# The last chunk's output blocks share PSUM banks, a bias moves to VectorE, and the softmax sums become halving additions

## The chip, the cores and the metric

The kernel runs on one core of a Trainium2 chip. The metric is the device time of one execution in microseconds. A difference of about 0.2%, some 0.4 us, is what a measurement of this kernel can tell from no change.

## The reference

```python
S, D, F, H = 2048, 640, 1536, 32          # Dh = 20; window W = 8, dilation 2
xn  = layernorm(x)                        # A_x; no scale, no shift
q, k, v = split(xn @ wqkv)                # 32 heads of 20
# position s attends to s, s-2, ..., s-14; those before 0 are masked
attn = softmax(einsum("bhsd,bhswd->bhsw", q, kg) * Dh**-0.5)
A    = einsum("bhsw,bhswd->bhsd", attn, vg).reshape(B, S, D) @ wo
B    = gelu(xn @ w1 + b1) @ w2 + b2       # tanh form
out  = x + A + B                          # bf16 in and out
```

## The kernel before

The 2048 rows are cut into four chunks of 512 (`NCH`, `CH`), each of four blocks of 128 rows (`BPC`). For each chunk the kernel normalizes the rows, turns them (a transposing DMA from SP for chunks 1 to 3, the `td` pieces named `tc`), and makes q, k and v by matmuls (`pj`, and `hj` in chunk 0) which ScalarE copies out of PSUM (`pc`, `hc`). The columns of a q, k or v tile are reordered so that a head has four rows in each of five tiles of 128.

Attention of a window of eight is done elementwise on VectorE. `qk` multiplies q by shifted k into two buffers, `half[0]` and `half[1]`, four window positions each. Some of the five tiles are then added up on VectorE, `pa` (two tiles onto two others) and `pb` (another tile onto the first), and `lg` sums over the rest with matmuls against `head_of`, 32 output rows each, into the PSUM tile `L`. How many tiles VectorE adds is `LEVEL[n]`: at level 0, 1, 2 and 3, `lg` has 40, 24, 16 and 8 matmuls. Then the softmax: `m` (maximum), `mx` (subtract), `ex` (exp on ScalarE), `ss` (sum over the eight positions), `ri` (reciprocal as Exp(-Ln) on ScalarE), `at` (multiply). `xd` and `xs` spread the result over the rows of a head by DMAs from SP, for blocks 0, 1 and 2, 3. `av` multiplies by v, `ad` and `ot` add up into `oT`. Chunk 0's softmax goes in two halves of 64 columns (`PARTS`).

The MLP's first product is `f1`, its GELU on ScalarE `ge`. ScalarE changes its table between GELU and the exp/ln functions.

For chunks 0 to 2 the output is made turned: `t{n}{s}{pc}` accumulates 128 output columns `s` over the 12 tiles of the MLP (pc 0 to 3) and the five of `oT` (pc 4), `u` adds the bias on ScalarE, `ut` turns it by a DMA from SP, `ud` adds it into the output by an accumulating DMA from POOL. x was stored there before (`xp`). For chunk 3 the output is made straight, by blocks of 128 rows: `o3{bl}{pc}` accumulates 512 low columns (`lo`) and 128 high ones (`hi`) in two PSUM tiles, ScalarE copies both (`oc`), and POOL adds them into the output (`od`), where `xp3` had stored x and `xb3` had added the bias b2. The last block, `LASTB`, is not stored first: `xl` adds b2 to its x in SBUF, `o33` makes its low columns, `oclo` adds x to them on VectorE and stores them from SP, `ohi` makes the high columns, 17 matmuls, `ochi` adds x and `ochd` stores them from ScalarE's queue.

PSUM has three pools: `psA`, four buffers (tag `acc`, for the projections and `f1`), `psO`, two (tag `o`, for the output), and `psL`, one of two banks (tag `L`, for the logits).

The order of all this on TensorE, VectorE, ScalarE and SP is written out by hand: `ORDER` is a list of 609 pieces, and each engine's queue gets its instructions in that order and runs them in that order. POOL's queue is left to the framework. Waits between engines are put in by the framework, tile by tile.

The end of the list before:

```python
... t244 u24 o312 ut23 o313 ud22 ud23 ot3 o320 o321
o322 o323 o324 oc32 od32 ut24 o314 oc31 od31 o300 o301 o302 o303 o304 o332 o333 o334 ud14 ohi ud24 oc30 od30 oclo ochi
ochd
```

Of the kernel before, what the change touches and what calls it, by code (L numbers as in the profile page):

```python
# [42 lines left out]
tp01a gb3 tp01b tc01a tc01b gb4 gd gc0 ge tb b1 hj102 gc1 ho st02a st02 st03a hc102 gc4 st03 hj101 rs02 xn02 rs03 xn03  # L43
st10a st12a st13a st11a hc101 st12 hj100 hc100 hj200 tp02 tc02 tp03 tc03 pk st13 hj201 hc200 st11 st10 hj202 hc202
hj012 hc012 hc201 rs1 rc1 hj112 hc112 xn12 tc12 xn10 hj210 qk000 hj011 hc011 tc10 hj110 hc110 qk001 hj010 hc010 hc210
hj111 hc111 qk011 qk010 pa011 pa001 xn11 tc11 xn13 hj211 hc211 f10_5 tc13 f10_4 ge0_4 ge0_5 f10_0 ge0_0 f10_7 f10_10
pj113 pc113 pj103 pj111 ge0_10 pj101 pc111 pj114 ldx ge0_7 pa000 pc101 pa010 lg0 mask m0a ld2 pc103 pj102 pc114 pad11
su21 mx0a ex0a pj112 pc112 m0b mx0b ss0a pc102 ex0b ri0a ss0b pj100 pc100 at0a ri0b at0b pj110 pj104 pc104 pc110 xd0
qk111 f10_2 ge0_2 su22 qk100 hj212 hc212 f10_6 ge0_6 pj121 su20 f10_1 pc121 su23 ldo f11_10 ge1_10 ng2 ge0_1 sq20
f11_5 f10_11 pj122 pc122 f10_3 qk110 sq22 t040 qk101 f11_0 t000 lg1 xp0 av010 ge0_3 sq21 xs0 ge1_0 sq23 rs2 f10_8  # L50
ge0_8 t001 m1 f11_3 rc2 xn23 tc23 ge0_11 av031 t041 mx1 av021 xn20 tc20 f11_7 av011 ge1_5 ge1_7 av001 ge1_3 xp1 f10_9
t042 t002 xn21 ge0_9 tc21 pj120 xn22 tc22 av030 av000 f11_9 ge1_9 pj124 ex1 av020 ss1 pc120 pc124 pj123 pc123 ad00 ri1
t043 f11_2 t003 pj204 at1 pc204 xd1 su31 ad01 pad12 ad02 ot0 pj200 pc200 pj201 pc201 av101 xp2 pj212 su30 pc212 pj220
pj213 pc220 pc213 pj223 pc223 pj211 su33 pc211 pj203 su32 ng3 sq33 pad21 av100 sq31 pj202 f11_6 t004 u00 av110 xs1
av130 t044 av120 av131 av121 t010 av111 t011 t012 t013 u04 t020 t014 sq32 pc203 pc202 pj221 sq30 rs3 rc3 ad11 u01 ut00
ad10 ad12 t030 pj210 pc221 t031 t021 t022 ut01 ge1_2 pj214 xn33 tc33 t032 t033 t034 xn31 tc31 ge1_6 pj224 t023 t024
f11_8 ot1 pc214 pad22 pc210 qk201 qk211 qk210 xn30 tc30 f12_9 qk200 f11_1 pa210 pa201 xn32 ge1_8 u02 pa211 pa200 f11_4
ge1_1 t100 ge1_4 tc32 pj311 pc311 pb212 ud00 ud01 ge2_9 pj310 pc310 pad31 pj304 pc304 pj314 pc314 t101 pj300 pj324
pc324 ut02 pj303 f12_10 pb202 pc224 u03 pc303 xp3 pj301 pc301 xl ge2_10 pc300 f13_9 pj313 pc313 pj312 ud02 ut03 ud03
pj302 pc302 f13_6 ge3_6 pj323 lg2 pc312 qk300 m2 pc323 f11_11 ge1_11 f13_0 ge3_0 mx2 ut04 f13_11 ge3_9 ex2 pa300 ss2  # L60
qk310 ri2 at2 xs2 qk301 t130 t131 f12_1 ge2_1 ge3_11 t132 f13_10 qk311 t102 t103 f13_2 pa310 xd2 t104 pj320 pc320
f13_1 ge3_1 u10 ut10 ud10 f12_8 pa311 pa301 pb312 ge2_8 f13_8 ge3_8 t110 t133 t111 t112 t113 t114 u11 ge3_10 f12_5
pj222 pc222 pj321 pc321 pb302 lg3 av200 t134 u13 m3 av221 ge2_5 xb3 f12_11 t140 t141 t120 ut11 mx3 f12_2 ge3_2 av211
ex3 ss3 ri3 av220 ge2_2 f13_5 ge2_11 t142 t143 t121 t122 t123 f12_6 ge2_6 at3 xs3 f12_3 ge2_3 t124 u12 f12_7 pj322
ud04 av210 av201 av231 f12_0 t144 ge2_7 ge2_0 t200 av230 pc322 u14 ut12 ud11 f12_4 ge2_4 ge3_5 f13_4 ge3_4 o310 f13_7
ge3_7 t210 ad20 ad21 ad22 ot2 f13_3 t201 t202 pad32 av321 t203 ge3_3 o311 av331 ut13 av320 xd3 t204 u20 av300 ut14
ut20 ud12 ud13 t211 t212 t240 t213 t214 av311 u21 ud20 t241 t242 av310 av330 t220 t221 t222 t223 t224 u22 ut21 t243
av301 ad30 ad31 o330 o331 t230 ad32 t231 t232 t233 t234 u23 ut22 ud21 t244 u24 o312 ut23 o313 ud22 ud23 ot3 o320 o321
o322 o323 o324 oc32 od32 ut24 o314 oc31 od31 o300 o301 o302 o303 o304 o332 o333 o334 ud14 ohi ud24 oc30 od30 oclo ochi
ochd  # L70
# [4 lines left out]
def kernel(  # L75
# [544 lines left out]
    def do_o(n, bl, pc, parts):  # L620
        cs = slice(bl * P, (bl + 1) * P)
        if pc == 0 and "lo" in parts:
            for part in ("lo", "hi"):
                pool, tag = (psA, "acc") if bl % 2 else (psO, "o")
                tiles[part, n, bl] = pool.tile([P, CH], F32, tag=tag, name=part)
        lo, hi = tiles["lo", n, bl], tiles["hi", n, bl]
# [4 lines left out]
        for k, (lhs, rhs) in enumerate(srcs):
            first, last = pc == 0 and k == 0, pc == 4 and k == len(srcs) - 1
            if "lo" in parts:
                nc.tensor.matmul(lo[:], lhsT=lhs, rhs=rhs[:, 0:CH], start=first, stop=last)  # L634
            if "hi" in parts:
                nc.tensor.matmul(hi[:, 0 : D - CH], lhsT=lhs, rhs=rhs[:, CH:D], start=first, stop=last)  # L636

    def do_oc(n, bl):
        osb = outp.tile([P, D], BF16, tag="osb", name="osb")
        tiles["osb", n, bl] = osb  # L640
        nc.scalar.copy(osb[:, 0:CH], tiles["lo", n, bl][:])
        nc.scalar.copy(osb[:, CH:D], tiles["hi", n, bl][:, 0 : D - CH])

    def do_od(n, bl):
        b = n * BPC + bl
        nc.gpsimd.dma_start(out_sd[b * P : (b + 1) * P, :], tiles["osb", n, bl][:], accum_op=ALU.add)
# [41 lines left out]
    last = (NCH - 1, BPC - 1)  # L688

    def do_oclo():  # L690
        osb = outp.tile([P, D], BF16, tag="osb", name="osb")
        tiles["osb", last] = osb
        nc.vector.tensor_tensor(out=osb[:, 0:CH], in0=tiles["lo", *last][:], in1=x_sb[:, LASTB, 0:CH], op=ALU.add)
        nc.sync.dma_start(out_sd[LASTB * P :, 0:CH], osb[:, 0:CH])
# [4 lines left out]

    def do_ochi():  # L700
        osb = tiles["osb", last]
        nc.vector.tensor_tensor(
            out=osb[:, CH:D], in0=tiles["hi", *last][:, 0 : D - CH], in1=x_sb[:, LASTB, CH:D], op=ALU.add
        )

    def do_ochd():
        nc.scalar.dma_start(out_sd[LASTB * P :, CH:D], tiles["osb", last][:, CH:D])
# [41 lines left out]
    for n in range(NCH):  # L749
# [52 lines left out]
        for bl in range(BPC):  # L802
            final = n * BPC + bl == LASTB
            for pc in range(5):
                piece(f"o{n}{bl}{pc}", do_o, n, bl, pc, ("lo",) if final else ("lo", "hi"))
            if not final:
                piece(f"oc{n}{bl}", do_oc, n, bl)
                piece(f"od{n}{bl}", do_od, n, bl)
# [39 lines left out]
```

## Time and profile before

| | |
|---|---|
| median of 3 runs | 210.01 us (209.93 to 210.13) |
| the profiled execution | 210.03 us, span 208.0 us |
| TensorE busy | 203.5 us, 1164 matmuls |
| VectorE busy | 180.9 us, 141 instructions |
| ScalarE busy | 127.5 us, 234 instructions |
| POOL busy | 24.9 us, 37 instructions |
| first transpose to end of the last matmul | 5.46 to 204.82 us |

The span runs from the first instruction of the program to the end of its last; some 2 us of the execution lie outside it. In a group of instructions ("L433 DVE TENSOR_TENSOR half<-qT,kT ... x16 | 44.3, 2820 | 1.0") the line is that of the kernel's source, then come the engine, what it writes and reads, how often, the microseconds of all, the nanoseconds of one, and the engine's idle time before them with what ended it. Matmuls are pipelined: the next starts before the row of the last one ends, so the price of one is the distance between starts. PE is TensorE, PEld its weight loads, DVE VectorE, ACT ScalarE, SP the SyncE queue; a small q behind an engine is its sequencer, which issues DMAs.

### The profile page before, as it was taken

Reading aid. Unit: us, or ns where it says so; the run is one execution under the profiler, and the core shown is the slowest. Engines: PE = TensorE matmul, PEld = TensorE weight load, DVE = VectorE, ACT = ScalarE, POOL = GpSimd, SP = SyncE. Lnnn points to the kernel's source line nnn. Section 1 sums busy time; section 2 is a strip of 40 time slices with the busy share of each in tenths; the row PEclk is TensorE's granted clock in tenths of the full one; section 3 lists DMA queues with packets and bytes.
Section 4 is the critical chain, followed back from the end, with each engine's and each line's share of the span. In section 5 each row is a group of like instructions: output and inputs, shape, how many; then the busy total and the mean of one; then the engine's idle time right before and its main releaser. Section 6 shows DMA issues by size and latency. Waiting matters only on the chain.

```text
span 208.0 us, 2951 instructions
## 1 busy us (share of the span) xinstructions
PE 203.5 (98%) x1164; PEld 107.0 (51%) x1164; DVE 180.9 (87%) x141; ACT 127.5 (61%) x234; POOL 24.9 (12%) x37
## 2 busy tenths in 40 slices
PE   8999999999999999999999999999999999999993
PEld 3999754554445554444455544444444444445552
DVE  2598995999699999999999989999999999999201
...
GB/s 217 388 395 137 68 207 395 60 122 238 162 82 162 11 189 138 25 50 91 90 25 56 114 123 0 0 188 81 37 0 100 121 108 54 50 50 76 49 68 63
DMA packets 36863, 23.88 MB, mean 115 GB/s; under 512 B 24946, under 2 KB 34674, under 8 KB 36850
## 3 DMA queue, kind: packets, MB, share of 16 engines
...
q8 instruction: 9, 0.15, 0.3%
q14 instruction: 4, 0.03, 0.0%
...
## 4 chain that ended last, share of the span: by engine, by line
PE 66%; DVE 21%; ACT 9%; DMA 2%; issue 1%; DVEq 0%; ACTq 0%
PE T L673 17%; PE pps L336 15%; PE hps L599 13%; PE lo L634 7%; PE gps L380 7%; DVE half L433 5%; DVE half L587 4%; DVE sums L530 3%; PE idle L446 2%; ACT L173 2%; DVE half L465 2%; DMA xnT<-xn 2%; DVE half L578 2%; ACT hT L615 2%; PE hi L636 2%; PE gps L349 1%
## 5 line engine op out<-in xcount | busy, mean ns | idle before, releaser
L599 PE MATMUL hps<-xnT,w_sb 128*128 128x512 bf16 x240 | 56.9, 379 | 0.1
L433 DVE TENSOR_TENSOR half<-qT,kT 128x5120 bf16<-128x5120 bf16 x16 | 44.3, 2820 | 1.0 <-ACT vT L400 0.7
L673 PE MATMUL T<-hT,w_sb 128*128 128x512 bf16 x180 | 43.3, 379 | 0.0
L685 POOL DMA_DIRECT2D out_dram<-x_sb x15 | 19.5, 1357 | 172.8 <-DMA x_sb<-x_sb 168.7
L599 PEld LDWEIGHTS <-w_sb 128*128 128x128 bf16 x240 | 23.3, 98 | 28.2 <-issue 1.2
L615 ACT ACTIVATE hT<-hps,bT 128x512 bf16<-128x512 f32 x36 | 24.1, 687 | 7.3 <-PE hps L599 7.2
L673 PEld LDWEIGHTS <-w_sb 128*128 128x128 bf16 x180 | 17.6, 98 | 21.1
L578 DVE TENSOR_TENSOR half<-vT,ax 128x2560 bf16<-128x2560 bf16 x16 | 23.1, 1484 | 2.4 <-PE L L479 2.4
L676 ACT ACTIVATE x_sb<-T,bT 128x512 bf16<-128x512 f32 x15 | 10.3, 687 | 23.6 <-PE T L673 23.6
L578 DVE TENSOR_TENSOR half<-vT,x_sb 128x2560 bf16<-128x2560 bf16 x16 | 22.6, 1485 | 0.0
L587 DVE TENSOR_TENSOR half<-half,half 128x5120 bf16<-128x5120 bf16 x8 | 22.3, 2820 | 0.1
L673 PE MATMUL T<-oT,wo 128*128 128x512 bf16 x75 | 18.3, 379 | 0.3 <-DVE oT L592 0.3
L336 PE MATMUL pps<-xnT,wk_sb 128*128 128x512 bf16 x75 | 18.3, 379 | 0.0
L336 PE MATMUL pps<-xnT,wv_sb 128*128 128x512 bf16 x75 | 18.3, 379 | 0.0
L336 PE MATMUL pps<-xnT,wq_sb 128*128 128x512 bf16 x75 | 18.2, 379 | 0.0
L173 ACT ACT_TABLE_LOAD x12 | 15.4, 1283 | 0.9 <-PEq L832 0.7
L465 DVE TENSOR_TENSOR half<-half 128x2048 bf16<-128x2048 bf16 x12 | 13.9, 1217 | 0.0
L336 PEld LDWEIGHTS <-wv_sb 128*128 128x128 bf16 x75 | 8.8, 117 | 7.6
L336 PEld LDWEIGHTS <-wq_sb 128*128 128x128 bf16 x75 | 8.7, 118 | 7.7 <-issue 0.4
L336 PEld LDWEIGHTS <-wk_sb 128*128 128x128 bf16 x75 | 8.8, 117 | 7.5
L263 ACT ACTIVATE xn<-x_sb,nmr,rstd 128x640 bf16<-128x640 bf16 x12 | 10.6, 916 | 3.2 <-DMA xnT<-xn 2.3
L400 ACT CAST vT<-pps 128x512 bf16<-128x512 f32 x15 | 8.5, 589 | 6.1 <-PE pps L336 6.1
...
## 6 DMA issues: line engine op xcount, KB each, us to landing
w_sb<-in_B_w_dram SPq DMA_DIRECT2D x4, 960.0 KB, 10.3
...
```

Source lines behind the costliest of these rows:

```text
L173: nc.scalar.preload_act_table_set(name)
L336: nc.tensor.matmul(ps[:], lhsT=wqkv_p[which][:, ti, to, :], rhs=xnT[:, ti, :], start=(ti == 0), stop=(ti == KT - 1),)
L380: nc.tensor.matmul(ps[:, to - a, :], lhsT=wqkv_p[which][:, ti, to, :], rhs=tiles["xnT", 0][:, ti, pair * 2 * P : (pair + 1) * 2 * P], star ...
L433: nc.vector.tensor_tensor(out=half[h][:, :, :, cs], in0=q[:, :, at].unsqueeze(1).to_broadcast([P, W // 2, KT, 2 * P]), in1=window(k, h, at ...
L465: nc.vector.tensor_tensor(out=even, in0=even, in1=odd, op=ALU.add)
L578: nc.vector.tensor_tensor(out=half[h][:, :, :, cs], in0=window(qkv_tile(n, 2), h, cs), in1=ax_view(n)[:, j, ws, :].unsqueeze(2).to_broadca ...
L587: nc.vector.tensor_tensor(out=a, in0=a, in1=b, op=ALU.add)
L599: nc.tensor.matmul(ps[:], lhsT=w1_sb[:, ti, ft * P : (ft + 1) * P], rhs=tiles["xnT", n][:, ti, :], start=(ti == 0), stop=(ti == KT - 1),)
L615: nc.scalar.activation(hT, tiles["hps", n, ft][:], ACT.Gelu_apprx_tanh, bias=bT[:, ft : ft + 1], scale=1.0)
L634: nc.tensor.matmul(lo[:], lhsT=lhs, rhs=rhs[:, 0:CH], start=first, stop=last)
L673: nc.tensor.matmul(ps[:], lhsT=lhs, rhs=rhs, start=pc == 0 and k == 0, stop=pc == 4 and k == len(srcs) - 1)
L685: nc.gpsimd.dma_start(dst, src, accum_op=ALU.add)
```

## The change

The last two blocks of chunk 3 (`DIRECT = 2`) are both finished on VectorE and stored directly: x plus bias is added as PSUM is emptied (`direct`). `dc` does this for block 2 and `dd` stores it from SP. `xl` adds the bias for two blocks, `xp3` and `xb3` cover two, and `oc32` and `od32` are gone.

The high columns of two blocks share a bank. Those of blocks 0 and 1 lie in one `psA` tile. Block 3's low columns and the high columns of blocks 2 and 3 lie in one tile `tail` of the `psL` pool: the first bank holds the low columns, the second the two high parts. Only the first matmul in a bank has the start flag.

The softmax sums (`ss`) are three additions of halves in float32 in place of one reduction: four positions onto four, two onto two, one onto one. They are kept in the `attn` tile before `at` overwrites it, or, for chunk 0, in a part of `half[0]`.

`LEVEL[3]` is 3: VectorE adds one tile more in each half (`pb304`, `pb314`), and `lg3` has 8 matmuls.

`ORDER` is written anew throughout; the counts of the other pieces stay.

```diff
+DIRECT = 2
-LEVEL = (1, 0, 2, 2)
+LEVEL = (1, 0, 2, 3)
...
     def rows(n):
-        cs = slice(n * BPC, min((n + 1) * BPC, LASTB))
+        cs = slice(n * BPC, min((n + 1) * BPC, LASTB + 1 - DIRECT))
...
     def do_xl():
-        nc.vector.tensor_tensor(out=x_sb[:, LASTB, :], in0=x_sb[:, LASTB, :], in1=b2bc[:], op=ALU.add)
+        rows_ = x_sb[:, LASTB + 1 - DIRECT :, :]
+        nc.vector.tensor_tensor(
+            out=rows_, in0=rows_, in1=b2bc[:].unsqueeze(1).to_broadcast([P, DIRECT, D]), op=ALU.add
+        )
...
     def do_sum(n, i):
-        total = softmax_tile("sums", n, [P], F32)
-        nc.vector.tensor_reduce(
-            out=total[:, i, :], in_=tiles["e", n][:, i, :, :].rearrange("p w c -> p c w"), axis=AX.X, op=ALU.add
-        )
+        a, e = sums(n, i), tiles["e", n][:, i, :, :]
+        nc.vector.tensor_tensor(out=a, in0=e[:, 0 : W // 2, :], in1=e[:, W // 2 :, :], op=ALU.add)
+        for k in (2, 1):
+            nc.vector.tensor_tensor(out=a[:, 0:k, :], in0=a[:, 0:k, :], in1=a[:, k : 2 * k, :], op=ALU.add)
...
+    def out_ps(bl, hi):
+        if bl >= BPC - DIRECT and (hi or bl == BPC - 1):
+            whole = get("tail", lambda: psL.tile([P, W, P], F32, tag="L", name="tail"))[:].rearrange("p w c -> p (w c)")
+            return whole[:, CH + (bl % 2) * P : CH + (bl % 2 + 1) * P] if hi else whole[:, 0:CH]
+        pool, tag = (psA, "acc") if hi or bl == 1 else (psO, "o")
+        key = ("hi", bl // 2) if hi else ("lo", bl)
+        ps = get(key, lambda: pool.tile([P, CH], F32, tag=tag, name=key[0]))
+        return ps[:, (bl % 2) * P : (bl % 2 + 1) * P] if hi else ps[:]
...
             if "hi" in parts:
-                nc.tensor.matmul(hi[:, 0 : D - CH], lhsT=lhs, rhs=rhs[:, CH:D], start=first, stop=last)
+                bank = bl // 2
+                first = bank not in opened
+                opened.add(bank)
+                nc.tensor.matmul(
+                    out_ps(bl, True), lhsT=lhs, rhs=rhs[:, CH:D], start=first, stop=final, skip_group_check=True
+                )
...
+    def direct(bl, hi):
+        b = (NCH - 1) * BPC + bl
+        room = half[1][:].rearrange("p w t c -> p (w t c)")[:, (bl % 2) * D : (bl % 2 + 1) * D]
+        cs = slice(CH, D) if hi else slice(0, CH)
+        nc.vector.tensor_tensor(out=room[:, cs], in0=out_ps(bl, hi), in1=x_sb[:, b, cs], op=ALU.add)
+        return room, out_sd[b * P : (b + 1) * P, :]
...
+    def do_dc():
+        direct(BPC - 2, False)
+        tiles["dc"] = direct(BPC - 2, True)
+    def do_dd():
+        room, dst = tiles["dc"]
+        nc.sync.dma_start(dst, room)
```

The parts of the new order that matter here:

```python
... at0b ri0a at0a pc110 pj100 pc100 xd0 qk101
qk110 hj212 f10_1 ge0_1 f11_0 ge1_0 su21 xs0 ... lg1 ld2 ge0_3 f11_10 sq20 rs2 ldo xp0
... pb302 pb312 pb304 ... pb314 f13_8 ge3_8 lg3 ut04 xs2 av220 m3 mx3 ex3
... t244 u24 ot3 o332 o300 o301
o302 o303 o320 o321 o322 o304 ud14 ud22 o314 o323 ut23 ut24 ud23 o324 dc o333 o334 oclo ohi oc30 od30 oc31 od31 ochi
dd ud24 ochd
```

In the list of the changed program's instructions with their waits, the first matmul of `o333` and the first of `ohi` wait for VectorE; the list of before has no such wait at either place.

More of the change, by code (lines that the diff above doesn't have):

```diff
@@ L42 @@
 pad01 pad02 st00a st00 sum1 rs00 mean1 neg1 sq1 xn00a xn00b tp00a wa tp00b wb tc00a tc00b rs01 ga xn01a xn01b gb2
[L43 to L70, printed above, removed]
+tp01a gb3 tp01b tc01a tc01b gb4 gd gc0 ge tb b1 gc1 gc4 hj101 st03a st03 rs03 st02a st02 hj102 hc102 ho hj100 xn03
+rs02 xn02 st13a st11a st13 hj201 hc101 st12a st10a hc100 tp03 tc03 tp02 tc02 hj200 hj202 hc200 hc202 hc201 hj111 hc111
@@ new lines @@
+st12 st10 st11 rs1 rc1 hj112 hc112 xn12 tc12 hj210 xn10 tc10 hj110 hc110 hj211 hc211 pk qk000 hc210 qk001 pa000 pa010
+hj011 hj012 hc012 hc011 xn11 tc11 xn13 tc13 hj010 hc010 qk010 f10_7 qk011 ge0_7 f10_5 pad11 ge0_5 f10_10 ge0_10 pa001
+f10_4 f10_0 ge0_0 pj104 pj103 pa011 ge0_4 pj111 pc111 pj114 pj101 pc103 lg0 mask pc104 m0b pc114 pc101 ldx su22 mx0b
+ex0b pj112 pc112 m0a pj102 pc102 mx0a ex0a ss0b ri0b pj113 pc113 ss0a pj110 at0b ri0a at0a pc110 pj100 pc100 xd0 qk101
+qk110 hj212 f10_1 ge0_1 f11_0 ge1_0 su21 xs0 f11_3 ge1_3 su23 qk100 f10_2 hc212 ge0_2 su20 f10_9 f11_7 ge1_7 f10_11
@@ new lines @@
+ge0_11 ng2 f10_6 ge0_6 f10_8 sq21 ge0_8 f10_3 sq23 ge0_9 sq22 qk111 pj124 lg1 ld2 ge0_3 f11_10 sq20 rs2 ldo xp0 f11_9
+av010 m1 pc124 av031 rc2 xn23 xn20 pj121 t000 tc23 pc121 f11_5 ge1_10 tc20 av030 ge1_9 t040 t041 av011 t042 av021 mx1
+av000 xn22 tc22 ge1_5 av001 av020 xn21 tc21 ex1 ss1 ad00 xp1 pj122 pj120 pc122 t001 t002 pc120 f11_11 t043 ri1 at1
+ad01 ad02 xd1 t003 ot0 pj123 pc123 pad12 xp3 pad21 av111 pj202 pj221 pc221 pc202 pj200 xp2 pj212 pc212 av101 pj203
+pc203 pj210 pc200 su31 pc210 pj220 pj224 pc224 pc220 su33 xs1 pj222 su32 pj213 pj201 pc222 pc201 su30 ng3 av110 av100
@@ new lines @@
+av130 t044 u04 pj204 pc204 pc213 av121 sq33 pj211 sq30 av131 t010 av120 t011 t012 pj223 pc223 f11_8 t013 sq32 sq31 rs3
+rc3 t004 u00 xn33 tc33 t014 u01 pj214 pad22 t020 t021 t022 t023 t030 t031 t032 pc211 t033 xn32 tc32 t024 t034 ut00
+pc214 xn31 tc31 ge1_11 f11_6 ad10 ad11 ad12 ot1 xn30 qk201 qk211 pa210 f11_1 ge1_6 ge1_1 qk210 ge1_8 f11_4 f11_2 ge1_2
+qk200 pa211 pa200 pa201 f12_3 ge2_3 tc30 pj302 pc302 pj320 pj314 pc314 ge1_4 u03 pj303 pc303 pj301 pb212 pj312 pc312
+ud00 pb202 pc301 pj313 pc313 pc320 pj310 pj300 pc300 f13_5 pj304 ge3_5 pc310 pad31 pj311 f12_9 pc311 pc304 xl f13_9
@@ new lines @@
+ge3_9 ut01 ge2_9 u02 lg2 f13_4 f12_4 qk310 m2 f13_3 ge3_3 pa301 ut02 ut03 mx2 ex2 ud01 qk300 ss2 ri2 t100 t110 pj321
+t101 t102 pa300 at2 qk311 qk301 pa311 pa310 f13_2 pb302 pb312 pb304 pc321 t111 t112 t103 t104 pad32 ud02 t113 t114
+ge3_2 f13_6 xd2 ge3_4 pj324 f12_8 u11 pc324 ge2_8 ge3_6 f13_1 ge3_1 t120 f12_11 ge2_11 u10 t121 t122 f12_10 t123
+ge2_10 f12_7 ge2_7 f13_10 pb314 f13_8 ge3_8 lg3 ut04 xs2 av220 m3 mx3 ex3 av201 ut10 t130 t131 t132 ss3 av230 ud10
+t124 u12 ut11 f12_0 ud11 t133 t134 u13 ut12 ri3 ut13 xb3 t140 ud12 t141 t142 f12_5 t143 ge3_10 at3 xd3 pj323 pc323
@@ new lines @@
+av211 ge2_0 t144 ge2_4 u14 ut14 pj322 pc322 xs3 av221 av231 av200 av210 ad20 ad21 ad22 f13_0 ud13 ud03 f12_2 ge3_0
+o330 o310 ge2_2 ge2_5 f12_1 ge2_1 ot2 f12_6 ge2_6 av331 av321 av311 f13_11 t210 o311 f13_7 t211 t212 t213 t200 t201
+t202 t203 t204 u20 o331 ut20 t214 u21 ut21 ud20 ud21 t220 t221 t222 t223 av310 ge3_7 t224 u22 ut22 t230 t231 t232 t240
+t233 t234 u23 av330 t241 t242 t243 o312 ge3_11 o313 av301 av300 ud04 av320 ad31 ad30 ad32 t244 u24 ot3 o332 o300 o301
+o302 o303 o320 o321 o322 o304 ud14 ud22 o314 o323 ut23 ut24 ud23 o324 dc o333 o334 oclo ohi oc30 od30 oc31 od31 ochi
@@ L498, in softmax_tile, with attn_tile, sums @@
         return get((key, n), lambda: smp.tile([P, PARTS[n]] + [s // PARTS[n] if s == P else s for s in shape], dtype, tag=key, name=key))
+    scratch = half[0][:].rearrange("p w t c -> p (w t c)").bitcast(F32)
     def shifted(n, i):
-        cs, width = part(n, i)
         if PARTS[n] == 1:
             return tiles["L", n][:]
-        low = half[0][:].rearrange("p w t c -> p (w t c)").bitcast(F32)[:, 0 : W * P]
-        return low.rearrange("p (i w c) -> p i w c", i=PARTS[n], w=W)[:, i, :, :]
+        return scratch[:, 0 : W * P].rearrange("p (i w c) -> p i w c", i=PARTS[n], w=W)[:, i, :, :]
+    def attn_tile(n):
+        return get(("attn", n), lambda: smp.tile([P, W, P], BF16, tag="attn", name="attn"))
+    def sums(n, i):
+        if PARTS[n] == 1:
+            return attn_tile(n)[:].rearrange("p w c -> p (w c)").bitcast(F32).rearrange("p (w c) -> p w c", w=W // 2)
+        room = scratch[:, W * P : W * P + W * P // 2]
+        return room.rearrange("p (i w c) -> p i w c", i=PARTS[n], w=W // 2)[:, i, :, :]
     def do_max(n, i):
@@ L528, in do_sum @@
     def do_sum(n, i):
-        total = softmax_tile("sums", n, [P], F32)
-        nc.vector.tensor_reduce(
-            out=total[:, i, :], in_=tiles["e", n][:, i, :, :].rearrange("p w c -> p c w"), axis=AX.X, op=ALU.add
-        )
+        a, e = sums(n, i), tiles["e", n][:, i, :, :]
+        nc.vector.tensor_tensor(out=a, in0=e[:, 0 : W // 2, :], in1=e[:, W // 2 :, :], op=ALU.add)
+        for k in (2, 1):
+            nc.vector.tensor_tensor(out=a[:, 0:k, :], in0=a[:, 0:k, :], in1=a[:, k : 2 * k, :], op=ALU.add)
     def do_recip(n, i):
         rs = get(("rs", n), lambda: smp.tile([P, PARTS[n], P // PARTS[n]], F32, tag="m", name="rs"))
-        total = tiles["sums", n][:, i, :]
+        total = sums(n, i)[:, 0, :]
         table(LOG_SET)
@@ L542, in do_attn @@
         cs, width = part(n, i)
-        attn = get(("attn", n), lambda: smp.tile([P, W, P], BF16, tag="attn", name="attn"))
+        attn = attn_tile(n)
         nc.vector.tensor_tensor(
@@ L617, in do_ge, with do_o @@
         )
[L620 to L626, printed above, removed]
+    def out_ps(bl, hi):
[6 more added lines that the diff above has]
+        return ps[:, (bl % 2) * P : (bl % 2 + 1) * P] if hi else ps[:]
+    opened = set()
+    def do_o(bl, pc, parts):
+        n, cs = NCH - 1, slice(bl * P, (bl + 1) * P)
         if pc < 4:
@@ L631, in do_o, with do_oc, do_od @@
         for k, (lhs, rhs) in enumerate(srcs):
-            first, last = pc == 0 and k == 0, pc == 4 and k == len(srcs) - 1
+            final = pc == 4 and k == len(srcs) - 1
             if "lo" in parts:
-                nc.tensor.matmul(lo[:], lhsT=lhs, rhs=rhs[:, 0:CH], start=first, stop=last)
+                nc.tensor.matmul(out_ps(bl, False), lhsT=lhs, rhs=rhs[:, 0:CH], start=pc == 0 and k == 0, stop=final)
             if "hi" in parts:
-                nc.tensor.matmul(hi[:, 0 : D - CH], lhsT=lhs, rhs=rhs[:, CH:D], start=first, stop=last)
-    def do_oc(n, bl):
-        osb = outp.tile([P, D], BF16, tag="osb", name="osb")
[L640 to L646, printed above, removed]
+                bank = bl // 2
[4 more added lines that the diff above has]
+                )
+    def do_oc(bl):
+        osb = outp.tile([P, D], BF16, tag="osb", name="osb")
+        tiles["osb", bl] = osb
+        nc.scalar.copy(osb[:, 0:CH], out_ps(bl, False))
+        nc.scalar.copy(osb[:, CH:D], out_ps(bl, True))
+    def do_od(bl):
+        b = (NCH - 1) * BPC + bl
+        nc.gpsimd.dma_start(out_sd[b * P : (b + 1) * P, :], tiles["osb", bl][:], accum_op=ALU.add)
+    def direct(bl, hi):
+        b = (NCH - 1) * BPC + bl
+        room = half[1][:].rearrange("p w t c -> p (w t c)")[:, (bl % 2) * D : (bl % 2 + 1) * D]
+        cs = slice(CH, D) if hi else slice(0, CH)
+        nc.vector.tensor_tensor(out=room[:, cs], in0=out_ps(bl, hi), in1=x_sb[:, b, cs], op=ALU.add)
+        return room, out_sd[b * P : (b + 1) * P, :]
     def spent_x(i):
@@ L685, in do_ud @@
         nc.gpsimd.dma_start(dst, src, accum_op=ALU.add)
-    last = (NCH - 1, BPC - 1)
+    def do_dc():
[4 more added lines that the diff above has]
+        nc.sync.dma_start(dst, room)
     def do_oclo():
[L691 to L694, printed above, removed]
+        room, dst = direct(BPC - 1, False)
+        nc.sync.dma_start(dst[:, 0:CH], room[:, 0:CH])
     def do_ohi():
         for pc in range(5):
-            do_o(*last, pc, ("hi",))
+            do_o(BPC - 1, pc, ("hi",))
     def do_ochi():
[L701 to L704, printed above, removed]
+        tiles["hi"] = direct(BPC - 1, True)
     def do_ochd():
-        nc.scalar.dma_start(out_sd[LASTB * P :, CH:D], tiles["osb", last][:, CH:D])
+        room, dst = tiles["hi"]
+        nc.scalar.dma_start(dst[:, CH:D], room[:, CH:D])
     pieces = {}
@@ L713, in piece @@
         pieces[name] = lambda: fn(*args)
-    for name in "tb b1 mean1 ho ldx ld2 ldo xl oclo ohi ochi ochd mask pk".split():
+    for name in "tb b1 mean1 ho ldx ld2 ldo xl dc dd oclo ohi ochi ochd mask pk".split():
         piece(name, locals()[f"do_{name}"])
@@ L802 @@
         for bl in range(BPC):
-            final = n * BPC + bl == LASTB
             for pc in range(5):
[L805 to L808, printed above, removed]
+                piece(f"o{n}{bl}{pc}", do_o, bl, pc, ("lo",) if bl == BPC - 1 else ("lo", "hi"))
+            if bl < BPC - DIRECT:
+                piece(f"oc{n}{bl}", do_oc, bl)
+                piece(f"od{n}{bl}", do_od, bl)
     engines = {getattr(mybir.EngineType, e) for e in ("PE", "DVE", "Activation", "SP")}
```

## The prediction

> **What bounds the kernel now.** I read the page first, then the waits, the chain and the timeline of the last microseconds.
>
> ```profile
> PE 203.5 (98%) x1164; PEld 107.0 (51%) x1164; DVE 180.9 (87%) x141; ACT 127.5 (61%) x234; POOL 24.9 (12%) x37
> ...
> PE   8999999999999999999999999999999999999993
> PEld 3999754554445554444455544444444444445552
> DVE  2598995999699999999999989999999999999201
> ```
>
> TensorE is busy in every slice, so what counts is its queue: the work in it and the holes in it. VectorE is nearly as full until about 193 us and can open holes. The waits say how little it does:
>
> ```profile
> DVE osb L693 <- PE lo L634: 10.2, 1, 10.2
> ACT hT L615 <- PE hps L599: 7.2, 8, 1.6
> ...
> PE T L673 <- DVE oT L592: 0.3, 1, 0.3
> ...
> PE L L479 <- DVE half L470: 0.2, 1, 0.2
> ```
>
> ScalarE and VectorE wait for TensorE for many microseconds, TensorE for VectorE for tenths. The chain prices the matmuls:
>
> ```profile
> 34.17 1.41 PE L L479 x24
> ...
> 49.20 1.09 PE pps L336 x5
> ...
> 203.86 0.96 PE hi L636 x17
> ```
>
> A 512-wide matmul takes 0.216 us (1.09/5), a logits matmul 0.059 (1.41/24), a 128-wide one 0.056 (0.96/17), and a lo/hi pair 0.272. I multiplied these by the matmuls of each piece and compared the sums with the starts in the trace: from the first transpose at 5.46 to 204.82 TensorE loses about 2.0 us. The visible holes are about 0.3 at the start, 0.44 ahead of `t004` (the output product waiting for `ot0`; the 0.3 of the waits, since a matmul's row outlasts its turn), 0.34 ahead of `lg3` (waiting for `pb302`), 0.25 ahead of `f12_3` (GELU late behind the softmax logarithm and a table load) and some of 0.1. The end:
>
> ```profile
> 203.70 0.50 PE L636 MATMUL hi<-w_sb,wq_sb 128*128 128x128 bf16 x6
> 203.95 0.69 DVE L693 TENSOR_TENSOR osb<-lo,x_sb 128x512 bf16<-128x512 f32 x1 [10.19 <-PE lo L634]
> ...
> 204.84 0.29 DVE L702 TENSOR_TENSOR osb<-hi,x_sb 128x128 bf16<-128x128 f32 x1 [0.20 <-PE hi L636]
> 205.17 0.36 ACTq L707 DMA_DIRECT2D out_dram<-osb  x1
> ```
>
> The last block's high columns (L636) start at 203.70 while VectorE empties its low columns (L693): they overlap, because `lo` and `hi` are two tiles. After the last matmul come 0.2 us, one VectorE addition, a store, and the end of the span at 208.0.
>
> **The change, part by part.** The sum is against the profiled execution, 210.03 us with a span of 208.0; the median of the runs is 210.01, so I carry no correction.
>
> *Fewer logits matmuls.* `LEVEL[3]` goes from 2 to 3: `lg3` has 8 matmuls in place of 16. 8 x 0.059 = 0.47 us less on TensorE, all on the path.
>
> *VectorE before the tail.* Added: `pb304` and `pb314`, each 128x2048 bf16; the L470 rows take 1.22 and follow each other every 1.14, so +2.28. `xl` adds the bias for two blocks: the row of L308 took 0.48 for 640 elements, L470 1.22 for 2048, so about 0.82 for 1280, +0.34. The sums: a reduction L530 of 1024 elements took 1.92. In its place come three additions, of 512, 256 and 128 float32 results. Bounds: 1 result a cycle as in L516 (0.69 for 512) and L702 (0.29 for 128), which gives 0.69 + 0.43 + 0.29 and two short dependencies, 1.46; at twice the rate, as in L470, about 1.1. I take 1.46, since L516 too is of float32: -0.44 for each of chunks 1 to 3, -0.15 for chunk 0's halves. Together +2.28 + 0.34 - 1.47 = +1.15 us of VectorE. It costs nothing if TensorE has work in front of each handover, so I compare those.
>
> - `t044` waits for `ot0`. Ahead of it stand 249 512-wide matmuls, as many as before `t004` now; without the hole TensorE gets there at 81.4. `ot0` ended at 81.81 and loses 0.6 us of sums before it: 81.2. Hole 0 (0.4 if the sums save nothing).
> - `lg3` waits for the last `pb`. TensorE has 10 more 512-wide matmuls ahead of it: 145.22 + 2.16 = 147.4, or 146.6 if the earlier holes close. VectorE: 145.17 + 2.28 + 0.34 - 1.03 = 146.8, and only the second half of `lg3`, 0.24 later, needs it. Hole 0 to 0.2.
> - `t204` and `o304` wait for `ot2` and `ot3`. The pieces from `o304` on hold 7.6 us of matmuls, so TensorE reaches it near 196; `ot3` is due at 193.76 + 1.15 = 194.9. Covered by about 1 us; if that cover went, up to 1.15.
>
> *The new order.* ScalarE's queue is rearranged; its table loads stay 12. Tight places are those where GELU follows a softmax logarithm and a table load (1.28): `pj323` waits for `ge3_10` there as `f12_3` does for `ge2_2` now, so I keep that 0.25. On SP, `xd0` and `xs0` pass the loads of w2, wo and b2 (`ld2`, `ldo`): these are issued near 45 us in place of 27, and the first use, `t000`, moves from 52.9 to about 59. The w_sb loads took 10.3 to land: 55, no hole. On POOL, `xb3` passes all 15 transposed additions; it waits for the store of `xp3`, long issued by then, and `ud00` behind it has no early reader. Net for holes: -0.44 - 0.34 = -0.78, less new small waits; I take -0.6, bounds -1.3 (all but the start closes) and +1.0 (one handover goes wrong).
>
> *The tail.* `tail` is one tile in two banks: the low columns of block 3, and behind them the high columns of blocks 2 and 3. The listing of the changed program with its waits shows what this does to TensorE's queue: the first matmul of `o333`, and the first of `ohi`, now wait for VectorE. Neither did before. Their places in the semaphore's count are `dc`'s second addition and `oclo`.
>
> - `o333` stands behind `o324`. From `o324`'s end: 0.2 to VectorE (as at 204.84), 0.61 until the second addition starts (L516's 0.69 less an overlap of 0.08), 0.29 for it, 0.05 back to TensorE (`ot0` ended at 81.81, `t004` began at 81.86): 1.16 us in which nothing can pass, since all that is left, `o333`, `o334` and `ohi`, stands behind.
> - `ohi` stands behind `o334`: 0.25 (203.70 to 203.95), 0.69, 0.05: 0.99 us, where the two now overlap.
>
> Together +2.15 us; bounds 1.95 (each handover 0.1 shorter) and 2.4. The copies of block 2 leave ScalarE (0.59 + 0.27) and one accumulating DMA leaves POOL; both had time to spare. The added store `dd` goes on SP behind that of `oclo`: its 160 KB are issued 0.4 us after that one and about 0.7 before `ochd`, which still ends the span. 0.
>
> The Trainium skill, "PSUM — Partial Sum Buffer", section "PSUM bank collisions raise a hardware error", says to guard PSUM by bank and quadrant. By that rule `o333` and `ohi`, each in another bank than the one that VectorE is reading, would have no wait here, and the sum would lack the 2.15. The listing has both waits, so the sum keeps them.
>
> Sum: 210.03 - 0.47 - 0.6 + 2.15 = 211.1 us.
>
> **Rivals.**
>
> *Faster: the tail waits cost little.* If both were over when TensorE arrives, 210.03 - 0.47 - 0.6 = 209.0. It decides as soon as they cost less than 0.65 together. Against it: `dc` reads what the matmul just before `o333` finishes, and one VectorE addition of 512 elements from PSUM is a measured 0.69. 0.04.
>
> *All holes close.* -0.47 - 1.3 + 1.95 = +0.2: 210.2, not to be told from no change (this measurement tells about 0.2%, 0.4 us). 0.10.
>
> *VectorE or ScalarE late.* The cover at `lg3` is tenths, at `pj323` 0.3. If the additions save nothing, VectorE is 1.5 later from chunk 2 on, and one or two handovers open 0.5 to 1.3 each: 212 to 213, with 212.3 the middle. 0.20.
>
> *A slower TensorE clock.* Two stops of about 1 us near the end. The first ten 512-wide warm-up matmuls took 0.44 each in place of 0.216, so the clock can halve; if it did for the last 2.7 us of matmuls, 213.8. Against it: the granted clock is 1.00 through the 0.44 us hole and 0.93 only once the matmuls have ended. 0.03. The Trainium skill, "TensorE: Matmul & The Clock Gate", section "What's actually happening", has the clock fall after an idle window of about 3.4 us; by that rule it would not fall here.
>
> The forecast itself, 210.5 to 211.9, has 0.63.
>
> **How the numbers follow.** Faster is the first rival, 0.04. Same is the second and the lowest edge of the forecast, 0.11. Slower is the rest, 0.85. The range runs from the closed holes, 210.2, to the late handover, 212.6.
>
> **What would show it.** In the changed profile's waits, two new rows of about 1.2 and 1.0 us of TensorE (`tail`) on VectorE; in the last microseconds the high columns starting only after `oclo`; L544 and L546 summing to 1.4 to 1.5 a chunk; 88 logits matmuls; no wait of `T` on `oT` above 0.1. I am wrong if TensorE has no hole after `o324`, if the holes before 190 us add up to more than 2.5, or if an end other than `ochd`'s store closes the span.

## The result and the profile after

The changed kernel takes 211.61 us (median of 5 runs, 210.95 to 212.02), the kernel before 209.98 beside it (209.93 to 210.13). The ratio is 1.0072, 95% interval 1.0050 to 1.0093: slower by 0.7%. Ratios, here and below, leave out a run that lies over 1.5% above the fastest of its kernel; there is one, in e1. The profiled execution of the changed kernel is the shortest of the five: 210.95 us, span 208.8, last matmul at 205.70.

The engines on the page of the changed kernel:

```profile
PE 202.8 (97%) x1156; PEld 106.3 (51%) x1156; DVE 182.7 (87%) x155; ACT 126.3 (60%) x232; POOL 23.9 (11%) x36
```

TensorE has 8 matmuls less and is busy for 0.7 us less, and it ends 0.9 us later. The waits of the changed kernel, TensorE's and those of VectorE that matter below (us in total, times, longest):

```profile
DVE half L679 <- PE tail L655: 2.0, 1, 2.0
...
PE tail L655 <- DVE half L679: 0.9, 1, 0.9
PEld L483 <- DVE half L474: 0.8, 2, 0.4
...
PE tail L660 <- DVE half L679: 0.8, 1, 0.8
...
PEld L353 <- DMA wq_sb<-in_A_wqkv_dram: 0.5, 1, 0.5
DVE half L592 <- DMA x_sb<-attn: 0.4, 1, 0.4
```

The two rows of PE `tail` that wait for L679, VectorE's additions, are the two new waits. The row of `T` on `oT` is gone. Two others are new, and the prediction had neither: the first weight load waits for w_q, and VectorE waits for a transfer out of `attn`. The last microseconds (start, duration, instruction, in brackets the idle time before it and who ended it):

```profile
200.98 0.69 DVE L679 TENSOR_TENSOR half<-lo,x_sb 128x512 bf16<-128x512 f32 x1 [6.07 <-PE lo L655]
201.59 0.28 DVE L679 TENSOR_TENSOR half<-tail,x_sb 128x128 bf16<-128x128 f32 x1
201.92 0.81 PE L655 MATMUL tail<-w_sb,wk_sb 128*128 128x512 bf16 x3 [0.92 <-DVE half L679]
202.56 1.24 PE L655 MATMUL tail<-wo,oT 128*128 128x512 bf16 x5
203.84 0.69 DVE L679 TENSOR_TENSOR half<-tail,x_sb 128x512 bf16<-128x512 f32 x1 [1.98 <-PE tail L655]
204.56 0.35 SPq L732 DMA_DIRECT2D out_dram<-half  x1
204.59 0.49 PE L660 MATMUL tail<-w_sb,wq_sb 128*128 128x128 bf16 x6 [0.78 <-DVE half L679]
204.96 0.42 SPq L728 DMA_DIRECT2D out_dram<-half  x1
205.25 0.44 PE L660 MATMUL tail<-wo,oT 128*128 128x128 bf16 x5
205.73 0.29 DVE L679 TENSOR_TENSOR half<-tail,x_sb 128x128 bf16<-128x128 f32 x1 [1.20 <-PE tail L660]
206.06 0.36 ACTq L743 DMA_DIRECT2D out_dram<-half  x1
```

TensorE and VectorE take turns: both additions of `dc`, then `o333` and `o334`, then `oclo`, then `ohi`, then `ochi`. Before, `ohi` ran beside `oclo`.

I compared the starts of the pieces with the sum of their matmuls, as for the kernel before. `o333` starts 1.09 us late and `ohi` 0.94 (the rows say 0.9 and 0.8, since a matmul's row outlasts its turn). Everything ahead of them loses 1.35, against 2.02 before: the holes ahead of `t004`, `lg3` and `f12_3` are gone (all but 0.1 at `lg3`), and one of 0.41 has come at the first `ga`, the first projection. So the last matmul ends -0.47 - 0.67 + 2.03 = +0.89 us later, which is what the trace has (204.81 to 205.70). From `ochi`'s end to the end of the span it is 2.8 us, 2.9 before.

### The profile page after: what moved, and what is told of

Same layout as the page of the kernel before. It is cut to its first block, busy times and chain, and to the rows that moved or that the text cites. A ratio compares the mean times of both kernels' runs of the same rounds, so it can differ in the third digit from the quotient of the medians.

```text
span 208.8 us, 2953 instructions
## 1 busy us (share of the span) xinstructions
PE 202.8 (97%) x1156; PEld 106.3 (51%) x1156; DVE 182.7 (87%) x155; ACT 126.3 (60%) x232; POOL 23.9 (11%) x36
## 4 chain that ended last, share of the span: by engine, by line
PE 95%; DMA 1%; DVE 1%; ACT 1%; issue 0%
PE T L707 26%; PE hps L613 25%; PE pps L340 23%; PE gps L384 7%; PE lo L655 5%; PE L L483 2%; PE tail L655 2%; PE gps L353 1%; DMA x_sb<-in_A_x_dram 1%; PE tail L660 1%; PE hi L660 1%; DVE half L679 1%; PE tp L281 1%; ACT trash L222 0%; DVE xnT L286 0%; DVE xn L266 0%
## 5 line engine op out<-in xcount | busy, mean ns | idle before, releaser
L613 PE MATMUL hps<-xnT,w_sb 128*128 128x512 bf16 x240 | 55.2, 379 | 0.0
L707 PE MATMUL T<-hT,w_sb 128*128 128x512 bf16 x180 | 42.6, 379 | 0.0
L404 ACT CAST kT<-pps 128x512 bf16<-128x512 f32 x15 | 8.8, 584 | 5.7 <-PE pps L340 5.7
```

Source lines behind the costliest of these rows:

```text
L613: nc.tensor.matmul(ps[:], lhsT=w1_sb[:, ti, ft * P : (ft + 1) * P], rhs=tiles["xnT", n][:, ti, :], start=(ti == 0), stop=(ti == KT - 1),)
L707: nc.tensor.matmul(ps[:], lhsT=lhs, rhs=rhs, start=pc == 0 and k == 0, stop=pc == 4 and k == len(srcs) - 1)
```

## The experiments

Each ratio is against the kernel before, run on the same chip. Times are medians.

**e1, the changed kernel again.** No edit; it goes with e2, e3 and e4.

> The changed kernel once more, unchanged. Theory A (two waits on VectorE in the last 4 us set the loss): holes of 1.1 and 0.9 us ahead of o333 and ohi again, whatever the total. Its five executions spread over 1.1 us, those of the kernel before over 0.2. Theory B on the spread: something ahead of 195 us moves from run to run (a DMA that lands late, then VectorE, then a handover to TensorE); if this profile is slower than 210.95, its extra time stands as a new hole of TensorE ahead of 195 us. Theory C on the spread: the TensorE clock drops in the two stops; then the extra time stands after 200 us, with more than 0.216 us between 512-wide matmuls.

211.34 us (210.55 to 211.75, and one run of 214.35; the median of the other eleven is 211.26), ratio 1.0048 (1.0027 to 1.0069). The kernel before stays between 209.76 and 210.40 in 31 of its 32 runs beside these, so the wider spread belongs to the change. This profile, 211.59, shows one source of it:

```profile
DVE half L592 <- DMA x_sb<-attn: 1.5, 1, 1.5
PEld L483 <- DVE half L474: 1.3, 2, 0.9
...
PEld L340 <- DMA xnT<-xn: 0.7, 1, 0.7
...
PE L L483 <- DVE half L474: 0.4, 1, 0.4
```

VectorE loses 1.5 us to a transfer near 81 us. Set beside the other profile matmul by matmul, TensorE gets two holes from it: 0.33 us ahead of chunk 3's first projection, whose transposed `xn` comes later because VectorE's part of its statistics does, and 0.50 ahead of the logits of chunk 2. At those of chunk 3 nothing is left of it. The first matmul of `o333` comes 0.67 us later than in the other profile. The tail itself is the same to a hundredth: from the start of `dc` to the end of `ochi` 5.05 us in both.

**e2, the high columns in a tile of their own.** Those of blocks 2 and 3 share a `psA` tile; `tail` keeps only block 3's low columns.

```diff
-        if bl >= BPC - DIRECT and (hi or bl == BPC - 1):
+        if bl == BPC - 1 and not hi:
```

> The high columns of blocks 2 and 3 lie in a tile of their own (a psA buffer), the low columns of block 3 alone in tail. Then o333 has no wait on dc, and ohi waits for dc only, which is over by then. Theory A: both holes go, 2.05 us less than the changed kernel of the same call, that is about 209.5 against 211.6, and below the kernel before by 0.4 to 0.6. Rival: the end is set by something else (a store or an accumulating DMA): less than 1 us gained.

209.34 us, ratio 0.9970 (0.9949 to 0.9991): faster than before. The end of its timeline:

```profile
200.56 0.81 PE L655 MATMUL tail<-w_sb,wk_sb 128*128 128x512 bf16 x3
200.71 0.69 DVE L679 TENSOR_TENSOR half<-lo,x_sb 128x512 bf16<-128x512 f32 x1 [6.07 <-PE lo L655]
...
202.29 0.50 PE L660 MATMUL hi<-w_sb,wq_sb 128*128 128x128 bf16 x6
202.49 0.69 DVE L679 TENSOR_TENSOR half<-tail,x_sb 128x512 bf16<-128x512 f32 x1 [0.89 <-PE tail L655]
...
203.44 0.29 DVE L679 TENSOR_TENSOR half<-hi,x_sb 128x128 bf16<-128x128 f32 x1 [0.26 <-PE hi L660]
203.61 0.42 SPq L728 DMA_DIRECT2D out_dram<-half  x1
203.76 0.36 ACTq L743 DMA_DIRECT2D out_dram<-half  x1
```

`o333` starts 0.15 us ahead of `dc`, `ohi` 0.2 ahead of `oclo`: both waits are gone. From `dc`'s start to `ochi`'s end it is 3.02 us in place of 5.05. So the two waits cost 2.03 together. But the span ends 3.2 us after `ochi`, in place of 2.8: 0.4 us of the gain is lost behind the last matmul.

**e3, only block 2's high columns apart.** Block 3's stay in `tail`.

```diff
-        if bl >= BPC - DIRECT and (hi or bl == BPC - 1):
+        if bl == BPC - 1:
...
-                bank = bl // 2
+                bank = bl if bl >= BPC - DIRECT else 0
```

> Only block 2's high columns lie in a tile of their own; block 3's high and low columns still share tail. Theory A: the hole ahead of o333 goes (1.1 us), the one ahead of ohi stays (0.94): 1.1 us less than the changed kernel. Rival (the stop of VectorE at dc merely moves on to o334 and ohi): less than 0.5 us gained.

209.76 us, ratio 0.9983 (0.9964 to 1.0002). `o333` starts ahead of `dc`; `ohi` still waits:

```profile
203.37 0.49 PE L660 MATMUL tail<-w_sb,wq_sb 128*128 128x128 bf16 x6 [0.78 <-DVE half L679]
```

From `dc` to `ochi` 3.97 us: the wait ahead of `o333` is worth 5.05 - 3.97 = 1.08, that ahead of `ohi` 3.97 - 3.02 = 0.95. The medians (1.6 below e1, 0.4 above e2) are blurred by the spread of the runs and by e2's later end. `ohi` waits although its bank is not the one that `oclo` is reading, because both lie in one tile. The Trainium skill, "PSUM — Partial Sum Buffer", section "PSUM bank collisions raise a hardware error", asks for a guard by bank and quadrant; the runs show that these waits go with the tile, not with the bank.

**e4, the sums by reduction again,** in the changed kernel.

```diff
-        a, e = sums(n, i), tiles["e", n][:, i, :, :]
-        nc.vector.tensor_tensor(out=a, in0=e[:, 0 : W // 2, :], in1=e[:, W // 2 :, :], op=ALU.add)
-        for k in (2, 1):
-            nc.vector.tensor_tensor(out=a[:, 0:k, :], in0=a[:, 0:k, :], in1=a[:, k : 2 * k, :], op=ALU.add)
+        total = softmax_tile("sums", n, [P], F32)
+        nc.vector.tensor_reduce(
+            out=total[:, i, :], in_=tiles["e", n][:, i, :, :].rearrange("p w c -> p c w"), axis=AX.X, op=ALU.add
+        )
...
```

> The softmax sums are reductions again, all else as in the changed kernel. By the trace of the changed kernel the three additions of a chunk take 1.47 us in place of 1.9, so VectorE has 0.15 + 0.45 + 0.45 us more work ahead of lg3. Theory A with cover: VectorE reaches t044 0.6 later, lg3 1.0 later; the holes there grow from 0.1 to between 0.3 and 0.9 in sum, 0.3 to 0.9 us slower than the changed kernel. Rival (VectorE has cover): less than 0.2 us.

212.26 us, ratio 1.0092 (1.0065 to 1.0120). This can't be read as the price of the sums: the interval overlaps e1's, and the profile lost its time at the start.

```profile
7.50 1.03 PE L353 MATMUL gps<-xnT,wq_sb 128*128 128x128 bf16 x15 [1.51 <-DMA wq_sb<-in_A_wqkv_dram]
```

From this matmul to the start of `dc` it takes 194.84 us, and in the profile after 194.56. The slower sums cost 0.3 at the most there, most of it one hole of 0.23 ahead of `pj323`; the rest of them was hidden, as in this order VectorE waits for TensorE at several places. e11 asks the question from the other side.

**e5, the block that lands first is used first.** In the order, `av101` and `av100` (block 0) stand ahead of `av111` and `av110` (block 1), as they did before.

```diff
-... av111 ... av101 ... av110 av100
+... av101 ... av100 ... av111 av110
```

> The changed kernel with chunk 1's first four products in another order: block 0 (av101, av100) ahead of block 1 (av111, av110), as in the kernel before. Theory B (in the changed kernel VectorE waits after ot0 for the second transfer of xd1, 0.4 us in one profile and 1.5 in another, and hands this on to lg2 and lg3): no wait of half on the DMA x_sb<-attn above 0.2, no hole of TensorE ahead of lg2 and lg3 above 0.3 together; median 0.3 to 0.6 below the changed kernel's 211.34 to 211.61, executions within 0.6 of each other. Rival (the spread is that of the first loads, 0 to 1.2 us ahead of the first projection): spread and median as they were, within 0.2.

210.77 us, ratio 1.0044 (1.0029 to 1.0059). VectorE's wait for `attn` is gone. The median is 0.6 below e1's, but the two ratios can't be told apart, the runs still go from 210.57 to 211.44, and the profile has 0.7 us of the wait for w_q at the start.

**e6, `xp3` later.** `xp3` stands behind `pc303` in place of `pad12`, some 40 us later (109.93 in place of 70.38), and `xb3`, which waits for its store, goes with it.

```diff
-... pad12 xp3 pad21 ...
+... pad12 pad21 ...
...
-... pj303 pc303 pj301 ...
+... pj303 pc303 xp3 pj301 ...
```

> The changed kernel with the store xp3 issued where the kernel before has it, after pc303; xb3, which waits for it on POOL, then no longer starts at 73.9 us, together with xd1. If xb3 and xp3 are what makes xd1 late: the wait of half on x_sb<-attn goes or falls below 0.3, as in e5, median 0.3 to 0.6 lower. Rival (xp2, or the four transfers of xd1 and xs1 themselves): wait and median as they were.

210.78 us, ratio 1.0042 (1.0027 to 1.0056), and again no wait for `attn`. The runs still go from 210.47 to 211.54, as widely as those of the changed kernel, so this transfer can't be the only source of the spread. What stood in the way is seen in the transfers. In the changed kernel, the store of `xp3`, `xb3` and `xd1`, and then VectorE:

```profile
70.38 0.41 ACTq L302 DMA_DIRECT2D out_dram<-x_sb  x1
...
73.88 1.35 POOL L306 DMA_DIRECT2D out_dram<-b2bc  x1 [71.83 <-DMA out_dram<-x_sb]
73.90 4.58 SPq L577 DMA_DIRECT2D x_sb<-attn  x4
...
81.44 2.89 DVE L592 TENSOR_TENSOR half<-vT,x_sb 128x2560 bf16<-128x2560 bf16 x2 [0.44 <-DMA x_sb<-attn]
```

and in e1 and in e6 the same four transfers of `xd1`:

```profile
73.67 5.55 SPq L577 DMA_DIRECT2D x_sb<-attn  x4
```

```profile
73.70 4.12 SPq L577 DMA_DIRECT2D x_sb<-attn  x4
```

Alone, SP issues them in 4.12 us, the same as before the change. In the nine profiles where `xb3` starts at the same moment or up to 0.7 us ahead, it takes 4.6 to 5.6, and where block 1 is read first VectorE waits between nothing and 1.6 us (0.1 in e2, 0.4 in the changed kernel, 1.5 in e1). `xb3` suffers too: 4.7 us from issue to landing in e6, 7.9 in the changed kernel. The Trainium skill, "DMA: Bandwidth & Descriptors", section "Issuing engines are not separate DMA queues", says that transfers issued from different engines share the same 16 DMA engines and interleave; the trace agrees, with these numbers.

**e7, LEVEL[3] back to 2** in the changed kernel.

```diff
-LEVEL = (1, 0, 2, 3)
+LEVEL = (1, 0, 2, 2)
...
-... pb302 pb312 pb304 ... pb314 ...
+... pb302 pb312 ...
```

> The changed kernel with LEVEL[3] = 2: pb304 and pb314 (2.3 us of VectorE) gone, lg3 again 16 matmuls (0.47 us of TensorE more). Where VectorE has cover at lg3: +0.47 us. Where lg3 waits for VectorE, as in the profiles with holes there (0.1 in one, about 0.9 in the other): -0.4 to +0.4, and the holes ahead of lg3 gone.

211.76 us, ratio 1.0079 (1.0063 to 1.0094): the median is 0.4 above e1's, but the two intervals overlap. The profiles are clearer: from the start of `lg3` to its end TensorE takes 0.43 us more than in the changed kernel, the 8 logits matmuls. VectorE gains nothing from the two additions less:

```profile
147.40 1.49 DVE L592 TENSOR_TENSOR half<-vT,ax 128x2560 bf16<-128x2560 bf16 x1 [3.43 <-PE L L483]
```

In the changed kernel this instruction starts at 147.37 after waiting 0.94. The additions fill time in which VectorE would wait for `lg3`.

**e8, e2 and e5 together.**

> High columns of blocks 2 and 3 in a tile of their own, and block 0 ahead of block 1 in chunk 1's products. If both gains are separate: 2.0 us from the first and 0.3 from the second, 209.0 us, 0.9 below the kernel before (ratio 0.9955). Rival (TensorE was waiting anyway): as e2, 209.3.

209.26 us, ratio 0.9974 (0.9957 to 0.9991), 0.1 below e2 and not to be told from it. SP's issue takes 5.48 us here, since `xb3` is where it was, but VectorE doesn't wait for it. The runs still go from 208.68 to 210.96, so the spread has another source as well.

**e9, e2 with the store `dd` right behind `dc`,** ahead of `oclo`'s.

```diff
-... o324 dc o333 o334 oclo ohi oc30 od30 oc31 od31 ochi dd ud24 ochd
+... o324 dc dd o333 o334 oclo ohi oc30 od30 oc31 od31 ochi ud24 ochd
```

> High columns of blocks 2 and 3 in a tile of their own as in e2, and the store `dd` moved in the order from the end to right behind `dc`, so that it stands ahead of oclo's store on SP. In e2 the span ended 3.27 us after ochi's addition, where it had been 2.86 before the change and 2.77 after it: dd's 160 KB were issued 0.15 us ahead of ochd and their packets lay in front of ochd's. Theory: with dd issued about 0.7 us sooner its packets are gone when ochd's come; the end falls back to 2.8 us behind ochi and the time to 209.34 - 0.45 = 208.9. Rival: all three stores wait for the same 16 engines and it is the sum of their bytes that counts; then the end stays 3.2 us behind ochi and the time at 209.3. A second rival: oclo's store, now behind dd's, becomes the last to land: 209.2 to 209.5.

209.49 us, ratio 0.9966 (0.9942 to 0.9990). The median doesn't show the gain. The profiled run, 209.99, has the `attn` wait with 1.6 us, and TensorE loses 0.6 us ahead of `lg2` and 0.3 ahead of chunk 3's first projection. The end of the span shows it: it comes 2.8 us after `ochi` again, in place of e2's 3.2. So `dd`'s packets had stood ahead of `ochd`'s.

**e10, e9 with `xp3` late as in e6.**

> e9, and xp3 put at the later place of e6. If the changes add up, this is the fastest version here: e9's 208.9, and no wait of VectorE for xd1 (0.4 to 1.5 us of VectorE in the runs of the changed kernel, of which only what is left at lg2 and lg3 counts, 0 to 0.7). Theory: 208.6 to 208.9, with less spread than e2 (208.92 to 209.81 without its one far run). Rival: e8 took the same wait away by the order of av and gained nothing over e2; then this is e9's time.

208.60 us (208.48 to 208.69), ratio 0.9926 (0.9907 to 0.9946): faster than both kernels, and the spread of 2 us in e9 is down to 0.2. Only `xp3` moved between the two, and all six runs are below the fastest of e9's twelve. That the move takes away the whole spread is not shown: e6 made the same move and kept 1.1 us. VectorE runs straight from `ot0` into `av111`, and the last microseconds have no turn-taking:

```profile
200.78 0.69 DVE L679 TENSOR_TENSOR half<-lo,x_sb 128x512 bf16<-128x512 f32 x1 [6.08 <-PE lo L655]
...
201.70 0.35 SPq L728 DMA_DIRECT2D out_dram<-half  x1
202.36 0.50 PE L660 MATMUL hi<-w_sb,wq_sb 128*128 128x128 bf16 x6
202.56 0.69 DVE L679 TENSOR_TENSOR half<-tail,x_sb 128x512 bf16<-128x512 f32 x1 [0.89 <-PE tail L655]
...
203.51 0.29 DVE L679 TENSOR_TENSOR half<-hi,x_sb 128x128 bf16<-128x128 f32 x1 [0.26 <-PE hi L660]
203.84 0.36 ACTq L743 DMA_DIRECT2D out_dram<-half  x1
```

TensorE's holes are 1.16 us in all, against 2.02 before.

**e11, the kernel before with the halving sums alone** (`do_sum` as changed, its tiles with it).

```diff
-        total = softmax_tile("sums", n, [P], F32)
-        nc.vector.tensor_reduce(
-            out=total[:, i, :], in_=tiles["e", n][:, i, :, :].rearrange("p w c -> p c w"), axis=AX.X, op=ALU.add
-        )
+        a, e = sums(n, i), tiles["e", n][:, i, :, :]
+        nc.vector.tensor_tensor(out=a, in0=e[:, 0 : W // 2, :], in1=e[:, W // 2 :, :], op=ALU.add)
+        for k in (2, 1):
+            nc.vector.tensor_tensor(out=a[:, 0:k, :], in0=a[:, 0:k, :], in1=a[:, k : 2 * k, :], op=ALU.add)
```

> The kernel before with one part of the change alone: the softmax sums by three halving additions. Theory, by the prediction's terms: VectorE is 0.6 us earlier at ot0 and 1.03 earlier at the last pb302, so the 0.44 us hole ahead of t004 and the 0.34 ahead of lg3 close: 210.0 - 0.78 = 209.2 at best, and no wait of T on oT above 0.1. Rival: the freed VectorE time goes into other waits of VectorE (for TensorE, for the DMAs xd and xs) and the holes stay: 209.9 to 210.1.

209.08 us (208.95 to 209.15), ratio 0.9949 (0.9930 to 0.9969): 0.96 less, somewhat more than expected. `oT` is ready 0.5 us sooner than the kernel before had it (80.31 to 79.85 for the start):

```profile
79.85 1.49 DVE L602 TENSOR_TENSOR oT<-half 128x2560 bf16<-128x2560 bf16 x1
```

The hole ahead of `t004` has closed, that of `lg3` is down to 0.10, and the 0.25 ahead of `f12_3` has closed too: 0.44 + 0.24 + 0.25 = 0.93. The third hangs on the sums as well, since ScalarE's logarithm, and the table load and the GELU behind it, wait for `ss3`. e4 shows the same in the new order: with the reductions back, 0.23 us of it returns ahead of `pj323`.

**e12, the kernel before with LEVEL[3] alone.**

```diff
-LEVEL = (1, 0, 2, 2)
+LEVEL = (1, 0, 2, 3)
...
-... pb312 ... pb302 lg3 ...
+... pb312 pb314 ... pb302 pb304 lg3 ...
```

> The kernel before with another part alone: LEVEL[3] is 3, and pb314 and pb304 stand right behind pb312 and pb302 in the old order. Theory: lg3 loses 8 matmuls, 0.47 us, but VectorE, which was already the last at lg3 by 0.34, comes 2.28 us later, of which the second half of lg3 hides 0.24 at most: 210.0 - 0.47 + 2.0 to 2.3 = 211.5 to 211.8, and a wait of lg3's matmuls or weight loads on VectorE of over 2 us. Rival: VectorE had waits of its own ahead of pb302 that swallow part of the 2.28: 210.0 to 211.0.

212.41 us, ratio 1.0119 (1.0094 to 1.0144): 2.4 us slower, more than expected. The wait and the additions:

```profile
PEld L479 <- DVE half L470: 3.2, 1, 3.2
PE L L479 <- DVE half L470: 2.7, 1, 2.7
```

```profile
142.86 4.88 DVE L470 TENSOR_TENSOR half<-half 128x2048 bf16<-128x2048 bf16 x4
```

Four additions take 4.88 us where two took 2.36, so the two cost 2.52, not 2.28. `pb314` and `pb304` each add onto what the addition just ahead of them wrote, and they start 1.26 us after it; in the changed kernel the four alternate between the two halves and follow each other every 1.14. The hole ahead of `lg3` grows from 0.34 to 2.86, that of `f12_3` by 0.22, less 0.47 of matmuls. The same edit that costs 2.4 us here costs nothing in the changed kernel, where e7 shows it to save 0.43.

## Why the prediction was right, point by point

Its sum was 211.1; the profiled run has 210.95, the median 211.61. The terms of the sum are those that the runs show, but it fits this closely in part by luck, as the holes show. A few of its numbers slip without moving the sum: 1.92 - 1.46 is 0.46, not 0.44; the four steps of the first wait add up to 1.15, not 1.16; the warm-up matmuls are 0.43 apart, not 0.44; and the first use of w2 before is `t040` at 51.2.

- *Logits matmuls, -0.47.* Right: 88 in the profile, and putting 8 back cost TensorE 0.43 in e7's profile.
- *VectorE's prices.* `xl` was put at 0.82 and took 0.817. The sums were put at 1.46 and take 1.47 from the start of the first to the end of the third; the rows of the three shapes in the groups of the changed kernel:

```profile
L544 DVE TENSOR_TENSOR attn<-e 128x512 f32<-128x512 bf16 x3 | 2.1, 684 | 0.0
...
L546 DVE TENSOR_TENSOR attn<-attn 128x256 f32<-128x256 f32 x3 | 1.3, 424 | 0.1
...
L546 DVE TENSOR_TENSOR attn<-attn 128x128 f32<-128x128 f32 x3 | 0.9, 292 | 0.1
```

  684 + 424 + 292 is 1.40, with a short gap ahead of each of the last two.
- *Holes, -0.6.* In the profiled run -0.67, and -0.86 where nothing disturbs them (e10). `t004` and `lg3` closed as argued. The 0.25 that I kept for `pj323` did not come: the faster sums take it away, as e4 and e11 show. What this gave, the wait for w_q, which I did not have, took back; that the total still fits is luck.
- *The tail, +2.15.* Right in place and mechanism, 0.1 too dear: 1.09 and 0.94 in the profile, 2.03 by e2. Each wait came out 0.05 to 0.07 below its price.
- *`dd`, 0.* Right for this kernel: `ochd` ends the span, 2.8 us after `ochi`. But that holds only as long as `ohi` is late. With the waits gone, `ochd` comes 0.15 us after `dd` and lands 0.4 us later (e2, e9).
- *"`ud00` behind it has no early reader."* This is the step that failed. I asked who waits for `xb3`, and nobody does; I did not ask what its bytes run beside. Moved ahead, it is issued at the same moment as `xd1`, and the new order reads block 1 of that transfer first, which lands second. VectorE loses up to 1.6 us there. TensorE loses nothing of it in the profiled run, where the wait is 0.4, and 0.8 to 0.9 us in e1 and e9, where it is 1.5 and 1.6. The median lies 0.66 above the profiled run; how much of that is this transfer, and how much the wait for w_q below, the runs do not show.
- *The rivals.* "The tail waits cost little" is excluded by e2 and e3. "All holes close" came true for the three holes that I had named, but the net is -0.67, not -1.3, and the price beside it stayed at 2.03. "VectorE late" was right that a handover could open in some runs, wrong on the cause: the additions save what they were priced at. The two stops did not lower the clock: behind them the matmuls follow each other every 0.216 and 0.056 us, as ahead of them. The granted clock, which I had argued from, is no proof of it: it reads 1.00 in the first 5 us too, where the warm-up matmuls are 0.43 apart.

The wait for w_q at the start (a hole of 0.41 us in the profiled run) stays open. It is in five of the eleven profiles with the new order, by 0.2 to 1.7 us, and in none of the three with the old one. It may well be the other source of the spread: seven of e4's eight runs lie between 212.15 and 212.45, its profile among them with 1.7 us of this wait, and the eighth is 210.62. The loads ahead of it are issued in the same order, and I ran nothing that tells chance from cause.
